# Queueing each operation one step after what it needs, loading tiles' y a slot sooner, and padding pools so that weights lie 64 bytes above

## The chip, the cores and the metric

The kernel runs on one core of a Trainium2 chip. The metric is the time of one execution on the device, in microseconds (us). The engines are named as the profile names them: PE is TensorE's matmul, PEld its weight load, DVE is VectorE, ACT is ScalarE, POOL is GpSimd, SP is SyncE, which here only issues DMAs.

## The reference, cut to what matters

Three blocks follow each other on an input of 4 x 3072 x 256 floats: a Fourier filter along the sequence, a channel mix with a token shift, and a gated layer of width 2048.

```python
X = np.fft.rfft(x, axis=1); Xr, Xi = X.real, X.imag
Yr = Xr @ w_r - Xi @ w_i + b_r
Yi = Xr @ w_i + Xi @ w_r + b_i
Yr = np.sign(Yr) * np.maximum(np.abs(Yr) - 0.01, 0.0)     # and Yi the same
y = np.fft.irfft(Yr + 1j * Yi, n=3072, axis=1)

prev = y moved one token down
xk = mu_k * y + (1 - mu_k) * prev;  xr = mu_r * y + (1 - mu_r) * prev
k = np.maximum(xk @ w_k, 0.0)
z = (1 / (1 + np.exp(-(xr @ w_r)))) * (k * k @ w_v)

h = z.reshape(12288, 256) @ w_in
out = (h * np.clip(h + 3, 0, 6) / 6) @ w_out
```

## The kernel before

**Products.** Every fp32 operand is split into a high part `h` (ACT copies it to the rounded type fp32r) and a low part `l` (DVE subtracts `h`); `three` then issues three matmuls for each product. A matmul has a stationary operand (the "weights" of the PE, 128 columns, loaded by a LDWEIGHTS ahead of it) and a moving one of 192, 256 or 512 columns. Either can be a tensor of weights of the model or data.

**Order.** All engines' queues are written out by hand: each engine executes its instructions in the order in which the program text issues them, and waits in that order. The Fourier filter is a stream of steps (generators that yield): `s1` and `mid` (which for each of 12 column groups j runs `s2`, `mix` and `ia`, through DRAM in between) and `ib`. After a first stretch with the stream alone, the channel mix runs beside it: per tile of 512 tokens one unit `u_r` and four `u_k`, each `u_k` followed two units later by its `u_v`; between units `feed` takes one step of the stream, and `ahead` prepares the next tile: it issues `load_y` (DMA of the tile's y), and takes steps of `prep` (ACT scales the shifted tokens into `xf`, DVE adds the others, ACT and DVE split it into `kh`, `kl`). A tile has ten slots. When the stream is empty the channel mix runs alone, and `decoder` steps decode the last block's weights: weights arrive as 64 bit floats and are turned into fp32 by DVE (L196, L200 to L204) and ACT (L197, L198), then split. L196 makes what L197 reads, and both are issued in the same step.

**Soft threshold.** `mix` ends with three DVE instructions on 128x512: add the bias (L361), `min(y + 0.01, 0)` (L362), `max(y - 0.01, that)` (L363); `split_y` and `ia` follow one step of j later.

**Last block.** The first tile (i = 0) runs in units `u_i` (12 matmuls of 512 columns, a gate on ACT and DVE, a split) and, three units later, `u_o` (24 matmuls of 256 columns). Beside them, from j = 3 on, `sums` and `split_s` prepare sums of weights (tile `sw`) and of data (tiles `th`, `tl`). The other 23 tiles run in 184 units `u_s` of 45 matmuls of 256 columns: 21 of a seven-product scheme into `rq` and `cc`, with `sw` or `wi` stationary, in four pieces with the 24 matmuls of an earlier unit's `u_o` between them. Into `oacc` the data `gh`, `gl` are stationary and the weights `wo` move.

**Where tiles lie.** Pools are laid out tile after tile, at 32 byte steps: `cst`, `kb`, `kw` (later `sp`) from the left, `fp` (later `w2`) up to the right end. Almost all tiles are multiples of 256 bytes long per partition, so a tile's offset modulo 256 is its pool's. In the program of the kernel before it is 32 for all of `kb`, `kw` and `sp`, 224 for all of `fp` and `w2`, 128 for `f1` and `fi`. The offset of the stationary operand less that of the moving one, modulo 256, is then 64 for `oacc` (`gh` 32, `wo` 224), 192 for products with `wi` stationary, and 0 for those with `sw`, for `mix`, `s2` and `ia`, and for the products `pr`, `pk` and `acc` of the channel mix.

Of the kernel before, what the change touches and what calls it, by code (L numbers as in the profile page):

```python
# [9 lines left out]
F32 = mybir.dt.float32  # L10
# [93 lines left out]
def fourier_mix_ffn_kernel(  # L104
# [36 lines left out]

    def ptile(name):
        return ps.tile([128, 1024], F32, tag="h", name=name)
# [15 lines left out]
    class Weights:  # L159
# [24 lines left out]
        def decode(self, staged, k, q, c, m):  # L184
# [3 lines left out]
            if self.wide:  # L188
# [7 lines left out]
                ts(au, high, 20, 0x7FF, op0=ALU.logical_shift_right, op1=ALU.bitwise_and)  # L196
                nc.scalar.activation(f, ai, AF.Relu, bias=top[:, 0], scale=-1.0)  # L197
# [5 lines left out]
                yield  # L203
# [6 lines left out]
            split(f, hi, lo)  # L210

    def decoder(jobs, stage):

        running = []
        for n in range(2 * len(jobs) + 4):
# [7 lines left out]

    def stage1():
        w = kb.tile([128, 1024], U32, tag="gh", bufs=3, name="stw")
        return w, kb.tile([128, 2, TOK], F32, tag="gl", bufs=3, name="stt")

    with tc.manual_schedule(engines=order):
        ff = ctx.enter_context(ExitStack())
        fp = ff.enter_context(tc.tile_pool(name="fp", bufs=1, side="right"))  # L230

        f1 = cst.tile([N1, 2, N1], F32R, name="f1")
        fi = cst.tile([N1, 2, N1], F32R, name="fi")
# [3 lines left out]
        half = cst.tile([128, 1], F32, name="half")  # L237
        top = cst.tile([128, 2, 1], F32, name="top")
        bias = fp.tile([128, 3, D], F32, name="bias")
# [9 lines left out]

        def load_chunks(upto):  # L250
            while head["load"] < min(len(chunks), upto) and chunks[head["load"]][1] in ready:
                n = head["load"]
                src, _, p = chunks[n]
                a = fp.tile([128, 2, D], F32, tag="a", bufs=5, name="a")
# [48 lines left out]
        def load_t(b, j):  # L303
# [3 lines left out]
            if b < B:  # L307
                t = fp.tile([128, 2, 640], F32R, tag="t", bufs=3, name="tt")
# [4 lines left out]
        def mid(b):  # L313
# [31 lines left out]
            def mix(j):  # L345
                xh, xl = xx.pop(j)
                p = ptile("mix")
                for g in range(2):
# [6 lines left out]
                    three(p[:, 256 * g : 256 * g + 256], pairs)  # L355
                y = fp.tile([128, 512], F32, tag="y", bufs=2, name="yf")
# [23 lines left out]

            for j in range(NP + 1):
                if j < NP:
                    s2(j)
# [5 lines left out]
                if j:  # L389
                    mix(j - 1)  # L390
                    fetch()
                    yield
                if 2 <= j < NP:
                    ia(j - 2)

# [72 lines left out]
        nc.vector.memset(half, 0.5)  # L468
        nc.vector.memset(top[:, 0], 1170.0)
        nc.vector.memset(top[:, 1], 254 * 2.0**23)  # L470

        def vectors():
# [7 lines left out]
            nc.vector.tensor_scalar(omu, mus, -1.0, 1.0, op0=ALU.mult, op1=ALU.add)  # L480

# [10 lines left out]
        def prep(i):  # L492
# [9 lines left out]
            for w in (1, 0):  # L502
# [14 lines left out]
                nc.scalar.activation(h, xf, AF.Copy)  # L517
                nc.vector.tensor_sub(l, xf, h.bitcast(F32))  # L518
# [74 lines left out]
        def u_i(i, j):  # L593
# [13 lines left out]
            split(g, h, l)  # L607
# [74 lines left out]
        def u_s(sp, pz, i, j, other, before, aside):  # L682
# [13 lines left out]
            cut = [len(other) * n // 3 for n in range(4)]  # L696
# [132 lines left out]
        for _ in range(3):  # L829
            next(preps)  # L830
            next(preps)
            next(fs)
# [20 lines left out]
        done2 = 0  # L853

# [7 lines left out]
        def ahead(i, slot):  # L862

            nonlocal preps
# [121 lines left out]
```

## Time and profile before

| | us |
|---|---|
| median of 3 runs | 2080.52 |
| lowest, highest | 2079.47, 2082.42 |
| the profiled execution | 2082.47 |
| its span, first to last instruction | 2080.7 |

The span is 1.8 us less than the profiled execution's own time, and that execution took 2.0 us more than the median. Times in the rows are counted from the span's start. Three stretches follow each other: the Fourier stream alone to about 170 us, stream and channel mix to about 780 us, the channel mix alone to about 1055 us, then the last block.

### The profile page before, as it was taken

How to read it: one execution, taken by the hardware profiler on the slowest of the kernel's cores; microseconds unless marked ns; L12 is line 12 of the kernel's file. 1: busy time of each engine (PE TensorE's matmuls, PEld its weight loads, DVE VectorE, ACT ScalarE, POOL GpSimd, SP SyncE). 2: the span in 40 equal slices, each digit the busy share in tenths (PEclk: the TensorE clock that was granted, in tenths of full speed). 3: DMA queues.
4: the chain of work that ended last, by engine and by line, in shares of the span. 5: the costliest groups of instructions: out<-in, count | busy, mean ns of one | idle time of the engine just before them, and what ended most of it. 6: DMA issues, size and time to landing. Idle time of an engine off the chain costs nothing.

```text
span 2080.7 us, 33798 instructions
## 1 busy us (share of the span) xinstructions
PE 1992.8 (96%) x13928; PEld 1844.5 (89%) x13928; DVE 1549.8 (74%) x1975; ACT 1323.2 (64%) x1917; POOL 35.0 (2%) x63
## 2 busy tenths in 40 slices
PE   6878999999999999889998999999999999999998
PEld 4867998898789888667787999999999999999998
DVE  3868667777677686767777777877787778777875
ACT  5556447555754565555646777777777777667775
POOL 0000000000000000000000000000000000000000
PEclk7978999999999999999999999999999999999999
DMA  9765447543653352122100001100110011001100
GB/s 265 240 205 165 123 114 228 163 142 115 216 170 111 95 179 65 63 75 77 51 31 24 29 23 29 32 21 23 30 32 21 22 31 32 21 22 31 32 11 21
DMA packets 106988, 175.85 MB, mean 85 GB/s; under 512 B 12945, under 2 KB 63314, under 8 KB 106834
## 3 DMA queue, kind: packets, MB, share of 16 engines
q1 hardware_dynamic: 96034, 141.76, 22.1%
q0 software_dynamic: 10480, 31.67, 5.7%
q8 instruction: 109, 1.79, 0.4%
q14 instruction: 45, 0.37, 0.1%
q10 hardware_dynamic: 320, 0.26, 0.0%
HBM read 110.35 MB, written 63.31 MB: 83 GB/s over the span
## 4 chain that ended last, share of the span: by engine, by line
PE 76%; DVE 14%; ACT 6%; issue 2%; DMA 2%; SPq 0%; ACTq 0%; DVEq 0%
PE oacc L776 24%; PE rq L776 15%; PE acc L156 8%; PE pk L156 7%; PE cc L776 6%; PE mix L156 5%; PE s L156 4%; DVE g L552 2%; DVE gl L553 2%; PE pr L156 2%; DVE xf L511 1%; PE ia L156 1%; DVE kl L518 1%; PE ib L421 1%; PE ib L420 1%
## 5 line engine op out<-in xcount | busy, mean ns | idle before, releaser
L776 PE MATMUL oacc<-wo_hi,gl 128*128 128x256 f32 x1536 | 426.7, 278 | 0.6 <-DVE gl L750 0.6
L776 PE MATMUL oacc<-wo_hi,gh 128*128 128x256 f32 x1536 | 427.1, 278 | 0.0
L776 PE MATMUL oacc<-wo_lo,gh 128*128 128x256 f32 x1536 | 425.4, 277 | 0.0
L776 PEld LDWEIGHTS oacc<-wo_hi,gl 128*128 128x128 f32 x1536 | 288.7, 188 | 1.0 <-DVE gl L750 0.8
L776 PEld LDWEIGHTS oacc<-wo_hi,gh 128*128 128x128 f32 x1536 | 288.5, 188 | 0.2
L776 PEld LDWEIGHTS oacc<-wo_lo,gh 128*128 128x128 f32 x1536 | 288.7, 188 | 0.0
L732 DVE TENSOR_TENSOR c<-rq,s 128x512 f32<-128x512 f32 x184 | 127.3, 692 | 184.2 <-ACT s L728 184.2
L745 DVE SCALAR_TENSOR_TENSOR g<-g,c 128x1024 f32<-128x1024 f32 x184 | 225.5, 1226 | 27.1 <-ACT g L744 17.4
L749 ACT ACTIVATE gh<-g 128x1024 fp32r<-128x1024 f32 x184 | 195.2, 1061 | 55.8 <-DVE g L745 55.8
L750 DVE TENSOR_TENSOR gl<-g,gh 128x1024 fp32r<-128x1024 f32 x184 | 223.7, 1216 | 1.2 <-ACT gh L749 1.2
L776 PE MATMUL rq<-th,sw 128*128 128x256 f32 x1104 | 217.4, 277 | 7.3 <-DVE g L606 7.3
L744 ACT ACTIVATE g<-c,half 128x1024 f32<-128x1024 f32 x184 | 211.5, 1150 | 4.1 <-DVE c L733 1.4
L712 ACT ACTIVATE s<-rq 128x512 f32<-128x512 f32 x184 | 109.9, 598 | 112.0 <-PE rq L776 111.5
L776 PEld LDWEIGHTS rq<-th,sw 128*128 128x128 f32 x1104 | 166.4, 188 | 7.5 <-DVE g L606 7.5
L156 PE MATMUL acc<-gl,wv_hi 128*128 128x512 f32 x384 | 153.8, 400 | 13.3 <-DVE gl L553 13.3
L547 ACT ACTIVATE g<-pk 128x1024 f32<-128x1024 f32 x96 | 97.6, 1016 | 106.5 <-PE pk L156 106.4
L156 PE MATMUL pk<-kh,wk_hi 128*128 128x512 f32 x384 | 152.8, 398 | 9.3 <-ACT kh L517 5.2
L776 PE MATMUL rq<-tl,sw 128*128 128x256 f32 x552 | 153.9, 279 | 2.8 <-DVE tl L679 2.8
L148 DVE TENSOR_TENSOR al<-a,ah 96x512 fp32r<-96x512 f32 (+1 forms) x176 | 114.9, 684 | 55.2 <-ACT ah L147 55.2
L156 PE MATMUL acc<-gh,wv_hi 128*128 128x512 f32 x384 | 153.2, 399 | 1.6 <-ACT gh L551 1.5
L156 PE MATMUL acc<-gh,wv_lo 128*128 128x512 f32 x384 | 152.2, 396 | 0.0
L156 PE MATMUL pk<-kl,wk_hi 128*128 128x512 f32 x384 | 151.9, 396 | 0.0
(150 smaller groups left out, 4953.0 us busy)
## 6 DMA issues: line engine op xcount, KB each, us to landing
tt<-in_tab_dram POOLq DMA_DIRECT2D x40, 640.0 KB, 4.9
yt<-sc_y SPq DMA_DIRECT2D x23, 608.0 KB, 3.9
a<-in_x_dram SPq DMA_DIRECT2D x64, 192.0 KB, 3.5
sc_a<-s1sb SPq DMA_DIRECT2D x32, 384.0 KB, 3.9
a<-sc_a SPq DMA_DIRECT2D x48, 256.0 KB, 3.2
sc_b<-iasb SPq DMA_DIRECT2D x48, 256.0 KB, 4.8
a<-sc_b SPq DMA_DIRECT2D x64, 192.0 KB, 3.1
sc_y<-ysb SPq DMA_DIRECT2D x32, 384.0 KB, 2.9
```

The lines of the kernel that those rows point to most:

```text
L148: nc.vector.tensor_sub(l, src, h.bitcast(F32))
L156: nc.tensor.matmul(o, a, c, start=first and i == 0, stop=last and i == n - 1, **kw)
L547: nc.scalar.activation(g, p, AF.Relu)
L552: nc.vector.tensor_mul(g, g, g)
L553: nc.vector.tensor_sub(l, g, h.bitcast(F32))
L712: nc.scalar.activation(s[:, 1:3].rearrange("p a n -> p (a n)"), rq, AF.Copy)
L732: nc.vector.tensor_add(c[:, 1::2], two(rq), s[:, 0:2])
L744: nc.scalar.activation(g, c, AF.Relu, bias=half, scale=1.0 / 6.0)
L745: nc.vector.scalar_tensor_tensor(g, g, 1.0, c, op0=ALU.min, op1=ALU.mult)
L749: lambda: nc.scalar.activation(h, g, AF.Copy),
L750: lambda: nc.vector.tensor_sub(l, g, h.bitcast(F32)),
L776: return lambda: nc.tensor.matmul(o, lhs, rhs, start=start, stop=stop, skip_group_check=True)
```

## The change

1. `decode`: L196 has a step of its own, the two ACT instructions come a step after it, the multiplication L204 moves up to the step of L200 to L202, and the split's ACT and DVE halves come in two steps. A job takes one step more.
2. `mix`: 0.01 is taken off the bias once, at the start; L362 becomes an ACT Relu with a bias tile (`lam2`), issued after `fetch`, and L363 moves to the start of the next j.
3. `prep`: the split's DVE half is a step of its own, so a tile takes 8 steps instead of 6. `load_y` is issued in slot 9 of the tile before where its y is written already, and the 8 steps then begin in slot 0 (to slot 7); otherwise as before.
4. First tile of the last block: the new sums of data come first, some DVE work (`between`) is put between the ACT and DVE halves of `u_i`'s split, part of the sums moves behind j = 7, and the last decode steps and `sp` stand ahead of `u_i` at j = 3. In the first `u_s`, all 24 matmuls of `u_o` come ahead of the 21.
5. `pad`: unused tiles of 32 to 192 bytes in the pools. Added up, they put `kb`'s `gh`, `gl` at 32, its other tiles (`xf` to `yt`) at 160, `wr`, `wk` and `sw` at 224, `wv` at 96, `th`, `tl` at 160, `f1` at 160, `fi` at 32, `a`, `ah`, `al`, `ev` at 96, `tt`, `Xh`, `Xl` at 32; `wi`, `wo`, `aw`, `yh`, `yl` stay at 224. For every product of high parts the stationary operand then lies 64 above the moving one, modulo 256.

```diff
 class Weights.decode
                 ts(au, high, 20, 0x7FF, op0=ALU.logical_shift_right, op1=ALU.bitwise_and)
+                yield
                 nc.scalar.activation(f, ai, AF.Relu, bias=top[:, 0], scale=-1.0)
                 nc.scalar.activation(ai, f, AF.Relu, bias=top[:, 1], scale=-(2.0**23))
                 yield
                 stt(au, high, 0x80000000, au, op0=ALU.bitwise_and, op1=ALU.bitwise_or)
                 ts(high, high, 0xFFFFF, 0x100000, op0=ALU.bitwise_and, op1=ALU.bitwise_or)
                 stt(f, low, 2.0**-32, high, op0=ALU.mult, op1=ALU.add)
-                yield
                 nc.vector.tensor_mul(f, f, a)
...
             yield
-            split(f, hi, lo)
+            nc.scalar.activation(hi, f, AF.Copy)
+            yield
+            nc.vector.tensor_sub(lo, f, hi.bitcast(F32))
 mid
                 nc.vector.tensor_add(y, p[:, 0:512], bs.rearrange("p g d -> p (g d)"))
-                nc.vector.tensor_scalar(m, y, LAM, 0.0, op0=ALU.add, op1=ALU.min)
-                nc.vector.scalar_tensor_tensor(y, y, LAM, m, op0=ALU.subtract, op1=ALU.max)
                 yy[j] = (y, yh, yl)
+                yield
+                nc.scalar.activation(m, y, AF.Relu, bias=lam2, scale=-1.0)
+                yield
+                nc.vector.scalar_tensor_tensor(y, m, -1.0, y, op0=ALU.mult, op1=ALU.max)
...
+            rest = iter(())
             for j in range(NP + 1):
+                next(rest, None)
                 if j < NP:
                     s2(j)
...
                 if j:
-                    mix(j - 1)
+                    rest = mix(j - 1)
+                    next(rest)
                     fetch()
+                    next(rest)
                     yield
 prep
                 nc.scalar.activation(h, xf, AF.Copy)
+                yield
                 nc.vector.tensor_sub(l, xf, h.bitcast(F32))
 ahead
-            if slot == late and i + 1 < len(seq):
-                b, t = seq[i + 1]
-                drain(b, (TOK * t + TOK - 1) // N1 // 4 if t else 0)
-                load_y(i + 1)
-                preps = prep(i + 1)
-            elif slot >= late + 2:
-                next(preps, None)
+            if i + 1 < len(seq) and i not in begins and (i + 1 in yt or slot == late):
+                begins[i] = (0, 8) if i + 1 in yt else (late + 2, 10)
+                if i + 1 not in yt:
+                    drain(*chunk(i + 1))
+                    load_y(i + 1)
+                preps, left = prep(i + 1), 8
+            if left and slot >= begins[i][0]:
+                for _ in range(-(-left // (begins[i][1] - slot))):
+                    next(preps, None)
+                    left -= 1
+            if slot == 9 and i + 2 < len(seq) and ("y", *chunk(i + 2)) in ready:
+                load_y(i + 2)
 u_i
-            split(g, h, l)
+            nc.scalar.activation(h, g, AF.Copy)
+            for f in between:
+                f()
+            nc.vector.tensor_sub(l, g, h.bitcast(F32))
 u_s
-            cut = [len(other) * n // 3 for n in range(4)]
+            cut = [len(other) * n // 3 for n in range(4)] if (i, j) > (1, 0) else [0, 0, 0, 0]
+            if (i, j) == (1, 0):
+                for f in other:
+                    f()
 the first tile of the last block
+                    x1 = split_s(sp, 1)
+                    beside = {
+                        3: ([x1[0][0]], [x1[0][1]]),
+                        4: ([x1[1][0]], [x1[1][1], c0[0][0]]),
+                        5: ([x1[2][0]], [c0[1][0]]),
+                        6: ([c1[0][0]], [c0[1][1], c0[2][0]]),
+                        7: ([c1[1][0]], [c1[1][1]]),
+                    }
-                    beside = {3: c0[:2], 4: c0[2:] + c1[:1], 5: c1[1:], 6: x1[:2], 7: x1[2:] + c2[:1]}
 start
+            nc.vector.tensor_scalar(bias, bias, LAM, None, op0=ALU.subtract)
 pads
+    def pad(pool, n):
+        pads.append(n)
+        pool.tile([128, n // 4], F32, name=f"pad{len(pads)}")
...
+        pad(cst, 32)
+        pad(cst, 128)
+        pad(cst, 64)
+            padded.append(pad(kb, 128))
+        pad_a, pad_t, pad_y = [128], [192], [192]
+        pad(kw_p, 64)
+        pad(kw_p, 128)
+                    pad(sp, 64)
+                    pad(sp, 192)
```

## Rows read from the trace of the kernel before

**Rows 1.** The page: busy time of each engine, share of the span, instructions.
```profile
PE 1992.8 (96%) x13928; PEld 1844.5 (89%) x13928; DVE 1549.8 (74%) x1975; ACT 1323.2 (64%) x1917; POOL 35.0 (2%) x63
```
**Rows 2.** Stretches: length, busy PE, PEld, DVE, ACT, POOL, then clock, DMA.
```profile
52.00:123.00 71.00, 62.43 (x484) 58.43 (x482) 64.02 (x105) 36.94 (x61) 7.74 (x13) 0.99 0.73 223
123.00:208.00 85.00, 67.90 (x324) 57.61 (x324) 60.97 (x96) 58.00 (x94) 1.61 (x3) 0.74 0.61 187
208.00:780.00 572.00, 567.47 (x3370) 500.15 (x3370) 413.06 (x542) 332.40 (x476) 21.39 (x37) 0.99 0.50 151
780.00:1092.00 312.00, 290.60 (x1289) 235.33 (x1287) 229.68 (x283) 175.60 (x208) 0.00 (x0) 0.98 0.19 60
1092.00:1107.00 15.00, 4.91 (x29) 4.41 (x28) 11.34 (x18) 6.32 (x8) 0.00 (x0) 0.69 0.13 35
1107.00:2071.00 964.00, 964.00 (x8311) 964.00 (x8309) 751.26 (x902) 685.17 (x1033) 0.00 (x0) 1.00 0.09 25
```
**Rows 3.** Waits, 780 to 1092 us: who for whom, us, times, longest.
```profile
ACT stt L197 <- DVE stt L196: 67.3, 16, 6.2
...
PE acc L156 <- DVE gl L553: 13.3, 14, 2.0
...
PE pk L156 <- ACT kh L517: 5.2, 1, 5.2
```
**Rows 4.** Timeline, 838 to 847 us: start, length, what, idle before and releaser.
```profile
838.88 0.72 ACT L197 ACTIVATE stt<-stt,top 128x512 f32<-128x512 int32 x1 [4.64 <-DVE stt L196]
...
843.48 1.23 DVE L552 TENSOR_TENSOR g<-g 128x1024 f32<-128x1024 f32 x1 [3.43 <-ACT gh L551]
...
846.02 0.50 PE L156 MATMUL acc<-gl,wv_hi 128*128 128x512 f32 x1 [1.79 <-DVE gl L553]
```
**Rows 5.** Timeline of ACT, 118 to 142 us.
```profile
123.53 0.72 ACT L197 ACTIVATE stt<-stt,top 128x512 f32<-128x512 int32 x1 [3.49 <-DVE stt L196]
```
**Rows 6.** Groups of instructions, 52 to 123 us: busy, mean ns, idle before.
```profile
L362 DVE TENSOR_SCALAR ym<-yf 128x512 f32<-128x512 f32 x12 | 5.2, 430 | 0.4
L197 ACT ACTIVATE stt<-stt,top 128x512 f32<-128x512 int32 x6 | 4.3, 724 | 15.5 <-DVE stt L196 15.5
```
**Rows 7.** The chain that ended last, 20 to 60 us.
```profile
42.69 0.09 DVE omu L480
```
**Rows 8.** DMA issues: form, count, KB, us to landing.
```profile
yt<-sc_y SPq DMA_DIRECT2D x23, 608.0 KB, 3.9
```
**Rows 9.** Waits of PE, 1092 to 1107 us.
```profile
PE rq L776 <- DVE g L606: 7.3, 1, 7.3
PE rq L776 <- DVE tl L679: 2.8, 1, 2.8
```
**Rows 10.** The chain that ended last, its longest pieces.
```profile
201.57 2.87 PE mix L156 x24
...
768.11 2.79 PE acc L156 x12
```
**Rows 11.** Timeline of PE, 1200 to 1206 us: one unit, and the next one's start.
```profile
1200.06 0.39 PE L776 MATMUL rq<-th,sw 128*128 128x256 f32 x2
...
1200.41 0.28 PE L776 MATMUL rq<-xh,wi_hi 128*128 128x256 f32 x1
...
1201.35 0.28 PE L776 MATMUL cc<-tl,wi_hi 128*128 128x256 f32 x1
...
1205.28 0.39 PE L776 MATMUL rq<-th,sw 128*128 128x256 f32 x2
```
**Rows 12.** Timeline of PE, 2066 to 2071.9 us: first and last of 17 matmuls.
```profile
2069.98 0.28 PE L776 MATMUL oacc<-wo_hi,gh 128*128 128x256 f32 x1
...
2071.79 0.28 PE L776 MATMUL oacc<-wo_hi,gl 128*128 128x256 f32 x1
```
**Rows 13.** Timeline of PE, 1068 to 1072 us: first and last of 24 matmuls.
```profile
1068.68 0.28 PE L776 MATMUL oacc<-wo_hi,gh 128*128 128x256 f32 x1
...
1071.39 0.28 PE L776 MATMUL oacc<-wo_lo,gh 128*128 128x256 f32 x1
```

More of the change, by code (lines that the diff above doesn't have):

```diff
@@ L222, in decoder @@
             yield
+    padded = []
     def stage1():
         w = kb.tile([128, 1024], U32, tag="gh", bufs=3, name="stw")
-        return w, kb.tile([128, 2, TOK], F32, tag="gl", bufs=3, name="stt")
+        t = kb.tile([128, 2, TOK], F32, tag="gl", bufs=3, name="stt")
+        if not padded:
+            padded.append(pad(kb, 128))
+        return w, t
     with tc.manual_schedule(engines=order):
@@ L394, in mid @@
                     ia(j - 2)
+            next(rest, None)
             def end(j):
@@ L591, in split_2, with u_i @@
             xt[i] = (h, l)
-        def u_i(i, j):
+        def u_i(i, j, between=()):
             xh, xl = xt[i]
@@ L828, in fourier_mix_ffn_kernel @@
         preps = prep(0)
-        for _ in range(3):
+        for n in range(4):
             next(preps)
             next(preps)
-            next(fs)
+            if n < 3:
+                next(fs)
         units = []
@@ L853, in fourier_mix_ffn_kernel @@
         done2 = 0
+        left = 0
         def decode_to(n):
@@ L862, in ahead @@
         def ahead(i, slot):
-            nonlocal preps
+            nonlocal preps, left
             if i + 1 == len(seq):
@@ L923, in fourier_mix_ffn_kernel @@
             if i == 0:
-                decode_to(max(done2 + 2, 2 * (j // 2 * 2 + 1) + 6, 2 * (8 + j) + 6))
-                u_i(i, j)
+                decode_to(max(done2 + 2, 2 * (j // 2 * 2 + 1) + 7, 2 * (8 + j) + 7))
+                if j == 3:
+                    decode_to(len(wi.jobs + wo.jobs) * 2 + 5)
+                    stage.close()
+                    sp = ctx.enter_context(tc.tile_pool(name="sp", bufs=1))
+                    pad(sp, 64)
+                    sw = [sp.tile([128, 4, 8, 128], F32R, name=f"sw{c}") for c in range(2)]
+                    pad(sp, 192)
+                    c0, c1, c2, c3 = (sums(sp, c) for c in range(4))
+                    x1 = split_s(sp, 1)
[6 more added lines that the diff above has]
+                    }
+                    both = lambda f, g: lambda: (f(), g())
+                    aside = [(both(c1[2][0], c2[0][0]), None), c2[1], (both(c2[2][0], c3[0][0]), None)] + c3[1:]
+                u_i(i, j, beside[j][0] if j >= 3 else ())
                 if lag:
@@ L932, in fourier_mix_ffn_kernel @@
                         f()
-                if j == 3:
-                    decode_to(len(wi.jobs + wo.jobs) * 2 + 4)
-                    stage.close()
-                    sp = ctx.enter_context(tc.tile_pool(name="sp", bufs=1))
-                    sw = [sp.tile([128, 4, 8, 128], F32R, name=f"sw{c}") for c in range(2)]
-                    c0, c1, c2, c3 = (sums(sp, c) for c in range(4))
-                    x1 = split_s(sp, 1)
-                    beside = {3: c0[:2], 4: c0[2:] + c1[:1], 5: c1[1:], 6: x1[:2], 7: x1[2:] + c2[:1]}
-                    aside = c2[1:] + c3
                 if j >= 3:
-                    for on_vector, on_scalar in beside[j]:
-                        on_vector()
-                        if on_scalar:
-                            on_scalar()
+                    for f in beside[j][1]:
+                        f()
             else:
```

17 lines of the change are left out of this document (15 added, 2 removed).

## The prediction

> **What bounds the kernel now.** The page's first part comes first: PE is busy for 96% of the span, DVE for 74%, ACT for 64% [rows 1]. That is an average over stages, so the stretches come next [rows 2]. From 1107 to 2071 us PE never pauses: only the pitch of its matmuls counts there. From 208 to 780 us it pauses for 4.5 of 572 us, so again the pitch. From 780 to 1092 us it is idle for 312 - 290.6 = 21.4 us though DVE is busy for 74% and ACT for 56%: nobody is full, so somebody stands in a queue for the wrong thing. From 52 to 123 us PE is idle for 8.6 of 71 us while DVE is busy for 90%. From 1092 to 1107 us PE works 4.9 of 15 us, at a granted clock of 0.69.
>
> The waits say where the 21.4 us come from [rows 3]: PE waits for DVE's `gl` (13.3 us) and once for `kh` (5.2 us), but the longest line is ACT waiting 67.3 us in 16 pieces for L196. The timeline shows that these are one thing [rows 4]. ACT stands 4.64 us at L197 until L196, the last thing in DVE's queue, is done; the Square behind it, which depends on nothing of the decoder, is late; DVE then stands 3.43 us for that Square; PE stands 1.79 us for the `gl` that follows. The two queues block each other in turn.
>
> **The change, part by part.**
>
> *Decode steps.* L196 goes into a step of its own. The instructions are the same; one order changes, 25 times. ACT's wait at L197 should go, and with it what stands behind it. In the stretch from 780 us the gain lies between 0 (the stall moves to another pair) and 21.4 us (all idle time of PE). DVE needs 229.7 us there [rows 2]; if PE's 21.4 us went, it would be 79% busy, so DVE has room. The single 5.2 us also belongs here: ACT's `kh` was queued behind L197. I take 16: some queueing stays at 79%. Between 123 and 208 us the first lines of PE's idle 17.1 us begin the same way: ACT stands 3.49 us at L197 [rows 5], ahead of the `yh` that the last `ia` of the first `mid` needs. I take 4, between 0 and 8; the rest is a DMA round trip through DRAM and a start at half clock. Staging buffers are held one step longer; a step lasts several us here, so the load's own time stays covered.
>
> *Soft threshold.* 48 times a DVE instruction of 0.430 us goes and an ACT instruction comes. Its nearest row is L197, a Relu on 128x512 with a bias tile, 0.724 us [rows 6]: 48 x 0.430 = 20.6 us off DVE, 48 x 0.724 = 34.8 us onto ACT. The Trainium skill speaks against this (ScalarE: Activation LUTs, Rules for kernel authors: relu, max and min belong on VectorE). The trace agrees on the single instruction, 0.724 against 0.430 us; by that rule alone the change would be worth -14 us of engine time. The sum goes by which engine is full: between 52 and 123 us DVE is at 90% and ACT at 52%, so 12 x 0.430 = 5.2 us come off the busiest queue. I take 5, between 0 (the latency from `mix` to `yl` sets the pace) and 8.6 (all idle). After 208 us, ACT gets 35 x 0.724 = 25 us on 332 of 572 us, and PE covers it. The new Relu waits for DVE's add, and behind it in ACT's queue stand `iasb` and the next unit's `g`; both need matmuls that PE does after `mix`, so they lose nothing while ACT keeps up; without that cover each Relu costs its 0.724 us. L363 stands ahead of the next `s2`, still a step before `split_y` needs it. The subtraction from the bias falls on the path: it follows `omu`, which is on the chain that ended last [rows 7], and `split` waits behind it. 768 elements by the row for 512: at most 0.430 x 1.5 = 0.65 us. I take -0.6.
>
> *Loads of y, and `prep`.* 23 DMAs of 3.9 us [rows 8] are issued one slot sooner on SP. No wait of PE is for `yt`; the 5.2 us wait was counted above. I cost it at nothing: `prep` begins a slot later and covers it; uncovered, each load would cost up to 3.9 us. SP may stand one slot longer for the store of the last y chunk, with loads of `a` queued behind it; five buffers of `a` cover that. The split into two steps takes DVE's wait for `kh` away and is in the terms above.
>
> *First tile of the last block.* PE's wait of 7.3 us for DVE's `g` and 2.8 us for `tl` [rows 9], and the slow clock that follows them, are the cost now. The gate itself is one instruction on ACT and one on DVE, each about as long as the 1.23 us of DVE's 128x1024 in [rows 4], and 24 products run beside them; so the 7.3 us are DVE's queue of sums, not the gate. The change takes two of DVE's sums behind j = 7, computes `tl` first, fills DVE's wait for `gh` with sums, and puts 24 matmuls (24 x 0.118 = 2.8 us) in front of what waits. At least these 2.8 us are covered; at most 10.1 us of waits and 4.9 x 0.31 = 1.5 us of slow clock. I take 9, since nothing but the gate should be left in front.
>
> *Pads.* Matmuls of one shape, 256 columns, do not run at one pitch. `mix`, stationary and moving at the same offset modulo 256 (difference 0): 2.87 / 24 = 119.6 ns [rows 10]. Products with `wi` (difference 192): 0.94 us over 8 steps, 117.5 ns [rows 11]. `oacc` (difference 64): 1.81 us over 16 steps, 113.1 ns [rows 12]. So where operands lie seems to matter, and 64 is the best seen. But the evidence is not clean: the same `oacc` products ran at 2.71 / 23 = 117.8 ns behind matmuls of 512 columns [rows 13]. For 512 columns, 2.79 / 12 = 232.5 ns [rows 10], about twice 113.1 and no room to gain: I put 0 there, at most 6 ns each.
>
> A unit `u_s` takes 1205.28 - 1200.06 = 5.22 us [rows 11], 116.0 ns on average over 45. With all at 113.1 it takes 5.09 us: 184 x 0.13 = 24 us gained. With all at 117.8, 5.30 us: 184 x 0.08 = 15 us lost. The pads leave `oacc` at its 64, and the six changes per unit between `oacc` and the scheme keep other differences (128 and 0), so not all 24 come: I take 12. For `mix` between 208 and 780 us (35 x 24 products): 840 x 6.5 ns = 5.5 us at most, with `ia` 1 more; at 117.8 ns, 1.5. I take 4, plus 1 for the waits in that stretch.
>
> What speaks against it: the Trainium skill (TensorE: Matmul & The Clock Gate, Step-by-step) says that PE reads moving and stationary operands through two independent ports, so that loading the next weights takes nothing from the running matmul. By that rule the pads do nothing; rows 10 to 12 disagree with it, rows 13 leave it open. It is the first rival.
>
> **The sum**, against the profiled execution's 2082.5 us: 16 + 4 + 5 - 0.6 + 9 + 12 + 5 = 50.4, so 2032 us. Against the median, 2 us lower, it would be 2030; I stay at 2032.
>
> **The rivals.**
>
> *The pads do nothing.* Pitch then depends on which matmuls come before, as rows 13 allow, and 12 and 4 fall away: 2048 us. For it: 117.8 and 113.1 ns on the same addresses. Against it: `mix` never leaves 119.6 at difference 0, and `oacc` holds 113 through long runs.
>
> *The stalls only move.* ACT still waits, now for L202's step or for the `xf` that DVE adds; of 16 + 4 + 5 only 5 come: 2052 us. For it: DVE also waits for ACT, as in the second line of [rows 4]. Against it: that line is itself an echo of L197, which is the longest wait of the stretch by far.
>
> *Everything comes.* 21.4 + 8 + 8.6 - 0.6 + 11.6 + 24 + 11 (5.5, 1 and the 4.5 of idle PE) = 84: 1998 us. It needs both the differences of 128 and 0 to be harmless and DVE never to be late.
>
> *Slower.* One mechanism, in the last block: the changes between differences 64, 128 and 0 throw PE into the slow pitch at every piece. The other gains are 16 + 4 + 5 - 0.6 + 9 = 33.4 us, and there are 184 x 45 = 8280 products, so it decides from 33.4 / 8280 = 4.0 ns more than 116.0, that is 120.0 ns on average, what `mix` has now. At 121 ns the time is 2082.5 - 33.4 + 41.4 = 2090 us.
>
> **How the numbers follow.** The forecast has 0.42, the pads without effect 0.25 (2048), stalls that move 0.14 (2052), everything 0.13 (1998), slower 0.06 (2090). The predicted time is the forecast's, 2032. The range from 2005 to 2060 holds the forecast with its bounds, both middle rivals and, of "everything", the part above 2005; outside stay some 0.18: most of "everything" and the slower case. A change of 0.2%, 4 us, is about the least that a measurement of this kernel tells from none. All cases but one end below 2076; for mixtures of rivals (pads that cost what half the stalls give) I keep 0.03 within 0.2%. So faster 0.90, same 0.03, slower 0.07.
>
> **What would show it.** Each step has its place: between 780 and 1092 us ACT's line for L196 should be nearly gone and PE's idle time down to about 5 us; between 52 and 123 us the steps of j should come every 5.5 instead of 6 us; the wait for `g` before the first `rq` should be under 2 us; a unit `u_s` should take 5.15 us, `mix` 2.75. If `u_s` still takes 5.22 us the pads failed; if PE's idle time after 780 us is 15 us or more, the order did.

## The result, and the profile after

The changed kernel takes 2059.4 us (median of 4 runs, 2058.5 to 2063.9), the kernel before 2081.4 us (2079.5 to 2082.4) beside it: a ratio of 0.9899, 95% interval 0.9884 to 0.9914. The change gains 22 us; the forecast was 50. The time lies in the range, 0.6 us from its upper end.

The page's first part of the changed kernel, PE's line, answers to [rows 1]:

```profile
PE 2000.5 (97%) x13928; PEld 1848.1 (90%) x13928; DVE 1529.6 (74%) x1929; ACT 1353.3 (66%) x1965; POOL 34.6 (2%) x63
```

PE has the same 13928 matmuls, a span 22 us shorter, and is busy for 7.7 us more. The stretches of the changed kernel, with the columns of [rows 2]:

```profile
52.00:123.00 71.00, 60.67 (x471) 58.76 (x470) 55.52 (x88) 43.03 (x72) 7.01 (x12) 0.93 0.67 209
123.00:208.00 85.00, 73.14 (x359) 61.12 (x358) 66.72 (x103) 62.83 (x101) 2.33 (x4) 0.80 0.67 208
208.00:780.00 572.00, 569.27 (x3384) 496.12 (x3383) 396.50 (x507) 357.74 (x511) 21.39 (x37) 1.00 0.49 150
780.00:1092.00 312.00, 306.94 (x1467) 252.20 (x1466) 255.08 (x320) 190.93 (x231) 0.00 (x0) 1.00 0.20 64
1092.00:1107.00 15.00, 14.85 (x127) 14.65 (x125) 13.79 (x19) 11.49 (x19) 0.00 (x0) 1.00 0.01 2
1107.00:2050.00 943.00, 943.00 (x8011) 943.00 (x8010) 722.44 (x861) 659.83 (x995) 0.00 (x0) 1.00 0.09 25
```

From 780 to 1092 us PE's idle time falls from 21.4 to 312 - 306.94 = 5.1 us, and from 1092 to 1107 us from 10.1 to 0.15. From 52 to 123 us it rises, from 8.6 to 10.3, though DVE is busy 8.5 us less. And in the last stretch PE never pauses in either kernel, but does 8011 products in 943 us where it did 8311 in 964: 8.50 in a microsecond, not 8.62.

The stretches are fixed in time, while the work moves through them. Between the same matmuls of both traces (times from the span's start):

| from the start of ... to ... | before, us | after, us | gained | forecast |
|---|---|---|---|---|
| the span, 12th `mix` (end of the first `mid`) | 115.8 | 119.9 | -4.1 | 4.4 |
| 13th `mix` | 85.6 | 78.0 | 7.6 | 4 |
| 48th `mix` (pitch of 208 to 780 us) | 510.5 | 506.7 | 3.7 | 5 |
| first `pi` (decode steps) | 340.4 | 321.8 | 18.6 | 16 |
| first `rq` of the second unit (first tile) | 59.1 | 47.8 | 11.3 | 9 |
| the end (183 units) | 969.3 | 984.4 | -15.0 | 12 |
| sum | 2080.7 | 2058.6 | 22.1 | 50.4 |

Two rows have the wrong sign. The last is one number 183 times. PE's timeline of the changed kernel, one unit and the next one's start, as in [rows 11]:

```profile
1202.16 0.40 PE L824 MATMUL rq<-th,sw 128*128 128x256 f32 x2
...
1203.58 0.28 PE L824 MATMUL oacc<-wo_hi,gh 128*128 128x256 f32 x1
...
1204.40 0.28 PE L824 MATMUL oacc<-wo_hi,gl 128*128 128x256 f32 x1
...
1207.46 0.40 PE L824 MATMUL rq<-th,sw 128*128 128x256 f32 x2
```

The unit takes 5.30 us, where it took 5.22, and `oacc`, whose addresses differ by 64 as before, runs at 0.82 / 7 = 117 ns, the pitch of [rows 13] and not that of [rows 12]. Of the 0.08 us that a unit lost, 0.06 are those of `oacc`: from the 21st unit on its 24 products take 117.5 ns on average where they took 114.9, though the pads left both of its operands where they were, modulo 256.

The first row shows in the waits of 52 to 123 us of the changed kernel:

```profile
ACT ym L391 <- DVE yf L388: 26.3, 8, 4.6
PEld mix L163 <- DVE yf L388: 9.7, 5, 2.1
PE mix L163 <- DVE yf L388: 8.8, 5, 2.0
```

and in one of these five waits, in the timeline from 96 us (DVE's rows from 98 to 102 us, the last product of `ia` among them, then the rows of ACT and PE that wait; the rest left out):

```profile
98.25 0.68 DVE L219 TENSOR_TENSOR wk_lo<-stt,wk_hi 128x512 fp32r<-128x512 f32 x1
98.86 0.68 DVE L208 SCALAR_TENSOR_TENSOR stt<-stw,stt 128x512 uint32<-128x512 uint32 x1
...
99.01 0.28 PE L163 MATMUL ia<-yl,tt 128*128 128x256 f32 x1
...
99.57 0.43 DVE L209 TENSOR_SCALAR stw<-stw 128x512 uint32<-128x512 uint32 x1
100.04 0.69 DVE L210 SCALAR_TENSOR_TENSOR stt<-stw 128x512 f32<-128x512 uint32 x1
100.76 0.69 DVE L211 TENSOR_TENSOR stt<-stt 128x512 f32<-128x512 f32 x1
101.37 0.42 DVE L203 TENSOR_SCALAR stt<-stw 128x512 uint32<-128x512 uint32 x1
101.71 0.68 DVE L388 TENSOR_TENSOR yf<-mix,bias 128x512 f32<-128x512 f32 x1
...
102.43 0.72 ACT L391 ACTIVATE ym<-yf,lam 128x512 f32<-128x512 f32 x1 [4.64 <-DVE yf L388]
102.45 0.39 PE L163 MATMUL mix<-aw_hi,Xh 128*128 128x256 f32 x1 [1.84 <-DVE yf L388]
...
103.06 0.58 ACT L407 ACTIVATE iasb<-ia 128x512 f32<-128x512 f32 x1
```

All six DVE operations of the decode stand in a row for 3.5 us. A new weight enters the decoder every second step, and the order before spread these operations over both of the two; queued one step later, those of a weight (L208 to L211) meet the remainder of the weight ahead (L219) and the first operation of the weight behind (L203), and the next step has none. `mix`'s addition L388 stands behind them, ACT stands 4.64 us at the new Relu L391 with an eviction (L407) behind it, and PE waits 1.84 us. The stall of L197 was taken away and another put in its place, in one stretch.

### The profile page after: what moved, and what is told of

The parts are those of the page before. It is cut to its first block, busy times and chain, and to the rows that moved or that the text cites. A ratio compares the mean times of both kernels' runs of the same rounds, so it can differ in the third digit from the quotient of the medians.

```text
span 2058.6 us, 33814 instructions
## 1 busy us (share of the span) xinstructions
PE 2000.5 (97%) x13928; PEld 1848.1 (90%) x13928; DVE 1529.6 (74%) x1929; ACT 1353.3 (66%) x1965; POOL 34.6 (2%) x63
## 4 chain that ended last, share of the span: by engine, by line
PE 80%; DVE 10%; ACT 5%; DMA 3%; issue 1%; SPq 0%; ACTq 0%; DVEq 0%
PE oacc L824 25%; PE rq L824 15%; PE acc L163 9%; PE pk L163 8%; PE cc L824 6%; PE mix L163 5%; PE s L163 4%; PE pr L163 2%; DVE g L591 2%; DVE gl L592 1%; PE ia L163 1%; PE ib L454 1%; PE pi L163 1%; PE ib L455 1%; DVE xf L549 1%
## 5 line engine op out<-in xcount | busy, mean ns | idle before, releaser
L824 PE MATMUL oacc<-wo_hi,gl 128*128 128x256 f32 x1536 | 431.6, 281 | 0.5 <-DVE gl L798 0.5
L824 PE MATMUL oacc<-wo_lo,gh 128*128 128x256 f32 x1536 | 430.4, 280 | 0.0
L824 PEld LDWEIGHTS oacc<-wo_hi,gh 128*128 128x128 f32 x1536 | 293.1, 191 | 0.2
L824 PE MATMUL rq<-th,sw 128*128 128x256 f32 x1104 | 222.1, 284 | 0.8 <-ACT s L771 0.6
L591 DVE TENSOR_TENSOR g<-g 128x1024 f32<-128x1024 f32 x96 | 117.4, 1222 | 79.8 <-ACT gh L590 79.8
L163 PE MATMUL pk<-kh,wk_lo 128*128 128x512 f32 x384 | 151.6, 395 | 0.0
```

The costliest lines, as they stand in the source:

```text
L163: nc.tensor.matmul(o, a, c, start=first and i == 0, stop=last and i == n - 1, **kw)
L591: nc.vector.tensor_mul(g, g, g)
L824: return lambda: nc.tensor.matmul(o, lhs, rhs, start=start, stop=stop, skip_group_check=True)
```

## Experiments

Each kernel was timed in turn with the kernel before on the same chip (medians 2081.5 to 2082.2 us); ratios are to that kernel.

### Order and pads apart

The new order with every tile at its offset of before: every pad 0 (and one of 224 bytes behind the constants, so that they take what they took).

```diff
-            padded.append(pad(kb, 128))
+            padded.append(pad(kb, 0))
...
-        pad_a, pad_t, pad_y = [128], [192], [192]
+        pad_a, pad_t, pad_y = [0], [0], [0]
...
-                    pad(sp, 64)
+                    pad(sp, 0)
```

> The new order alone, every tile at the offset it had before. Theory 1 (the pads cost): the pads lengthen a unit of the last block from 5.22 to 5.30 us (184 x 0.08 = 15 us) and the 512-column products from some 229 to 234 ns (2592 x 4.6 ns = 12 us), and give 1152 x 5.6 ns = 6 us back in mix; so this takes 2059 - 21 = 2038 us, a unit 5.22 us. Rival (the slow pitch comes from the new order of the first units of the last block, offsets do nothing): 2059 us, a unit 5.30 us.

The old order with the changed kernel's pads:

```diff
+            padded.append(pad(kb, 128))
...
+        pad(cst, 32)
         f1 = cst.tile([N1, 2, N1], F32R, name="f1")
...
+                    pad(sp, 64)
                     sw = [sp.tile([128, 4, 8, 128], F32R, name=f"sw{c}") for c in range(2)]
```

> The kernel before with the pads and nothing else. Theory 1: 2081 + 21 = 2102 us, a unit 5.30 us, mix at about 115 ns. Rival: 2081 us, a unit 5.22 us, mix at 120 ns.

The new order with the pads of the constants and of the first pool (`fp`) alone:

```diff
-            padded.append(pad(kb, 128))
+            padded.append(pad(kb, 0))
...
-        pad(kw_p, 64)
+        pad(kw_p, 0)
...
-                    pad(sp, 64)
+                    pad(sp, 0)
```

> The new order with the pads of cst and fp alone, so that mix, s2, ia and ib keep their difference of 64 and the channel mix and the last block lie as before. Theory 1: 2059 - 15 - 12 = 2032 us, a unit 5.22 us, mix at 115 ns. Rival: 2059 us.

The kernel just above, with the last block's stationary operands all at 32 and its moving operands all at 224 modulo 256 bytes (shown against the changed kernel; the channel mix has difference 0 throughout):

```diff
-            padded.append(pad(kb, 128))
+            padded.append(pad(kb, 192))
...
+                    pad(w2, 192)
                     wo = Weights(w2, w_out, 16, D, "wo")
```

> As the run with the pads of cst and fp alone, but in the last block every stationary operand lies at 32 and every moving one at 224, so the difference is 64 also where PE goes from one kind of product to the other; the channel mix has difference 0 throughout. If what spoils the last block are the differences of 128 and 0 at these changes: a unit of 45 x 113.3 = 5.10 us and 2032 - 22 = 2010 us. If a difference of 64 has two pitches whatever precedes it, and the last block settles in the slow one: a unit of 5.30 us and 2047 us.

The new order alone: 2044.6 us, 0.9817 (0.9799 to 0.9834), a unit at 5.220 us (PE's timeline, the starts of two units):

```profile
1202.47 0.39 PE L825 MATMUL rq<-th,sw 128*128 128x256 f32 x2
...
1207.69 0.39 PE L825 MATMUL rq<-th,sw 128*128 128x256 f32 x2
```

The pads alone: 2097.4 us, 1.0070 (1.0055 to 1.0085), a unit at 5.300. So the order gains 37 us and the pads lose 15 to 16, with either order; theory 1 had the pads at 21. With the pads of the first pool alone: 2041.0 us, 0.9801 (0.9787 to 0.9816): only those pay, by 3.6 us. `mix` has difference 64 in this kernel as in the changed one, and the mean from start to start after 200 us is 117.8 ns here and 114.4 there: one pair of addresses, two pitches, as in [rows 12, 13].

The fourth kernel was expected at 2010 us and took 2055.9, 0.9872 (0.9854 to 0.9890). Its first whole unit took 5.101 us, all products at 113.3 ns. In each of the next three PE waited once, for 0.2 to 0.5 us, and each wait turned the pitch over: 117.7 ns behind the first, 113.3 behind the second, 117.7 behind the third and from there to the end, every unit 5.300 us. Two waits in the opening unit, whose 24 `oacc` come ahead of its other 21 products, had left it at 113.3. PE's timeline, the starts of the first two whole units and then the three waits (the first one without a gap of its own: the second product of that row comes 0.22 us behind the first):

```profile
1070.72 0.39 PE L825 MATMUL rq<-th,sw 128*128 128x256 f32 x2
...
1075.83 0.39 PE L825 MATMUL rq<-th,sw 128*128 128x256 f32 x2
...
1078.17 0.50 PE L825 MATMUL rq<-th,sw 128*128 128x256 f32 x2
...
1085.60 0.51 PE L825 MATMUL rq<-th,sw 128*128 128x256 f32 x2 [0.21 <-ACT s L772]
...
1089.63 0.50 PE L825 MATMUL rq<-th,sw 128*128 128x256 f32 x2 [0.23 <-ACT s L761]
```

Differences of 128 and 0 between the pieces, my suspicion in the forecast, are gone here, and the slow pitch is not.

### What sets the pitch

The body of the kernel was replaced by series of products that nothing waits for:

```diff
+        for d in range(0, 64, 8):     # floats: differences 0, 32, ... 224 bytes
+            series(d, 512, 24, p); series(d, 256, 40, p)
+            for r in range(4):        # a wait for ACT, then
+                series(d, 256, 40 + r, p)
+            series(d, 192, 24, q)
```

> The body of the kernel is replaced by series of products that nothing waits for: stationary and moving operands whose addresses differ by 0, 32, 64, ... 224 bytes modulo 256, and for each difference 24 products of 512 columns, straight behind them 40 of 256, four more series of 40 to 43 of 256 each behind a wait of PE for ACT, and 24 of 192; nothing of the reference is computed. Theory A (the pitch is a matter of the difference and of how a series began): at difference 64 the products of 256 columns take 113.3 ns in some of the series and 117.7 in others, each the same from its beginning to its end, and at difference 0 they take 119 to 120; products of 512 columns take 229 ns at some differences and 234 at 64. Rival B (the two pitches belong to the order of the last block's products, not to the operands): every series of one difference has one pitch, 113 or 118 ns.

PE's timeline of it, a whole series in one row (start, time from the first start to the last end, what, count), first difference 0, then 64:

```profile
29.29 5.60 PE L150 MATMUL five<-mov,wts 128*128 128x512 f32 x24
34.73 4.95 PE L150 MATMUL run<-mov,wts 128*128 128x256 f32 x40
...
104.39 5.79 PE L150 MATMUL five<-mov,wts 128*128 128x512 f32 x24
110.02 4.87 PE L150 MATMUL run<-mov,wts 128*128 128x256 f32 x40
...
115.88 4.76 PE L150 MATMUL rs0x<-mov,wts 128*128 128x256 f32 x40
...
121.63 5.04 PE L150 MATMUL rs1x<-mov,wts 128*128 128x256 f32 x41
...
127.66 5.16 PE L150 MATMUL rs2x<-mov,wts 128*128 128x256 f32 x42
...
133.81 5.10 PE L150 MATMUL rs3x<-mov,wts 128*128 128x256 f32 x43
```

The 42 products of the third series at difference 64 take longer than the 43 of the fourth. Start to start, from the third product on, in ns:

| difference | 0 | 32 | 64 | 96 | 128 | 160 | 192 | 224 |
|---|---|---|---|---|---|---|---|---|
| 256 columns, lowest series | 119.7 | 118.3 | 113.3 | 117.4 | 118.7 | 119.8 | 117.7 | 116.7 |
| 256 columns, highest series | 120.0 | 118.5 | 117.8 | 118.7 | 120.1 | 120.0 | 117.8 | 117.8 |
| 512 columns | 226.7 | 233.4 | 233.4 | 234.3 | 232.4 | 233.8 | 229.5 | 233.5 |

Theory A holds: at 64 a series has 113.3 or 117.8 ns, from its beginning to its end. For 512 columns 64 is no good place: 6.7 ns worse than 0.

Does a product at difference 0 set the good pitch for those behind it, as `sw` seems to before `oacc` in the kernel before? Three kernels: the changed one with the sums back at 0; the best one so far (its decode is told below) with the first products' weights at 64 too; the same with one sum in four at 0.

```diff
-                    pad(sp, 64)
+                    pad(sp, 0)
```

> The changed kernel (2059.4 us) without the two pads of the pool that holds the sums of weights: the 12 products of a unit of the last block that have a sum as stationary operand stand at difference 0 to their moving operand again, the other 33 stay at 64, and nothing else is changed. Theory A: products at difference 0 throw those at 64 that follow into the fast pitch (121.7, 115.8, 114.2, then 113.3 ns, as in the kernel before), so a unit takes 5.18 us (5.16 to 5.20) where it takes 5.30: 2037 us (2033 to 2041). Rival B: the pitch of the others goes by their own operands alone and stays 117.7 ns: a unit takes 5.29 us or more, 2057 us (2054 to 2060).

```diff
+                    pad(w2, 128)
                     wo = Weights(w2, w_out, 16, D, "wo")
```

> As the kernel whose decode is spread further (2026.5 us; a unit of the last block takes 5.220 us with the sums at difference 0, the second products' weights at 64 and the first products' weights at 192), with the first products' weights moved to 64 by one pad of 128 bytes. Theory A: behind the sums they fall into the fast pitch too: a unit takes 5.18 us, 2019 us (2016 to 2023). Rival B: products at 64 that follow other products at 64 stay slow, as in the changed kernel: 5.25 us or more, 2032 us or more.

```diff
-                    sw = [sp.tile([128, 4, 8, 128], F32R, name=f"sw{c}") for c in range(2)]
+                    for c in range(2):
+                        s1 = sp.tile([128, 1, 8, 128], F32R, name=f"sw{c}a")
+                        pad(sp, 64)
+                        sw.append((s1, sp.tile([128, 3, 8, 128], F32R, name=f"sw{c}b")))
```

> As the kernel of theory A just before, and of the four sums only the first stays at difference 0 (three products at the start of a unit), the other three move to 64: 42 of a unit's 45 products are at 64. Theory A: three products at 0 are enough to set the fast pitch once in every unit: 5.12 us (5.11 to 5.15), 2009 us (2005 to 2015). Rival B: three are not enough, or the first wait behind them sets the slow pitch again: 5.25 to 5.30 us, 2032 to 2041 us.

Measured: 2058.5 us, 0.9884 (0.9870 to 0.9899), a unit at 5.280; 2025.2, 0.9724 (0.9708 to 0.9740), at 5.233; 2026.0, 0.9732 (0.9711 to 0.9754), at 5.227. The first came out at its rival's time; the other two lie between theory and rival, their units nearer to the rival's 5.25 us. Products behind a sum at 0 fell to 113.3 ns in some pieces of the unit and stayed at 117.6 in others, always the same pieces. My theory fell; what the pieces differ in is where both operands lie before and behind the step. So the unit's 45 products were run in their order, without waits, for 48 choices of places:

```diff
+        # moving: x at a, wo at 0; stationary: sums at a + ds, wi at a + dw, h at 64
+        for ds, dw in ((0, 192), (0, 64), (64, 64), (64, 192), (192, 64), (128, 64)):
+            for a in range(0, 256, 32):
+                for half in range(2):      # a wait of PE between the halves
+                    for u in range(3):
+                        unit(a, (a + ds) % 256, (a + dw) % 256, rq, cc, o, u == 0, u == 2)
```

> The body of the kernel is replaced by the 45 products of a unit of the last block in their order, for 48 choices of where the operands lie modulo 256 bytes, three units straight on and three more behind a wait of PE; nothing of the reference is computed. Theory C (the step of both operands' places from one product to the next sets the pitch, not the difference alone): the third unit of a choice takes the same time before and behind the wait, the five choices that ran in the kernel come out at 5.22, 5.23, 5.28, 5.30 and 5.10 or 5.30 us as there, and some other choice gives 5.15 us or less. Rival D (other work of the kernel sets the pitch: PSUM, the evictions of ACT, the waits): the five do not come out as in the kernel, and choices of one set of differences agree to 0.02 us.

PE's timeline of it: the starts of the second and third unit at the changed kernel's places (x at 192 above `wo`); then at those of the fourth kernel above (x level with `wo`), ahead of the wait and behind it; then with `wi` at 192 instead:

```profile
741.08 0.87 PE L159 MATMUL rq0a192s0w<-mov,wts 128*128 128x256 f32 x6
...
746.38 0.87 PE L159 MATMUL rq0a192s0w<-mov,wts 128*128 128x256 f32 x6
```
```profile
549.03 0.87 PE L159 MATMUL rq0a0s64w<-mov,wts 128*128 128x256 f32 x6
...
554.33 0.87 PE L159 MATMUL rq0a0s64w<-mov,wts 128*128 128x256 f32 x6
...
565.34 0.84 PE L159 MATMUL rq1a0s64w<-mov,wts 128*128 128x256 f32 x6
...
570.44 0.84 PE L159 MATMUL rq1a0s64w<-mov,wts 128*128 128x256 f32 x6
```
```profile
805.48 0.84 PE L159 MATMUL rq0a0s64w<-mov,wts 128*128 128x256 f32 x6
...
810.58 0.84 PE L159 MATMUL rq0a0s64w<-mov,wts 128*128 128x256 f32 x6
```

That is 5.30, then 5.30 and 5.10, then 5.10 us. The places of the kernel before give 5.220, those of the two kernels above 5.280 and 5.233: each as in its kernel. The places alone, with nothing else of the kernel running, give a unit's time in these four kernels, to 0.01 us. Over the 48 choices it goes from 5.10 to 5.32; choices with the same differences (sums at 64, `wi` at 192) reach from 5.10 to 5.31, so the difference of a product's two operands doesn't decide: what the product before it used counts too. `oacc` shows it best: it lies at the same two places in all 48 choices, and its mean pitch goes from 113.3 to 118.0 ns. One choice, that of the fourth kernel, has two times 0.2 us apart, and a wait chose; theory C, by which both should have been the same, misses there. Two other choices gave 5.10 on both sides of the wait; they ran in the kernel:

```diff
-            padded.append(pad(kb, 0))
+            padded.append(pad(kb, 192))
...
+                    pad(w2, 64)
                     wo = Weights(w2, w_out, 16, D, "wo")
...
-                    pad(sp, 0)
+                    pad(sp, 64)
```

> As the kernel whose decode is spread further (2026.5 us, a unit of the last block 5.220 us), with the places of the last block's operands by the series of units: all moving operands at 224, the stationary ones at 32 (sums, second products) and at 160 (first products' weights). Theory C (places alone): a unit takes 5.100 us as in the series, 2004 us (2000 to 2009). Rival D (the kernel's waits and evictions set the pitch too): the first wait sets the slow pitch and it stays, as with all of them at 32: 5.30 us, 2041 us; in between if only a part of the units keeps it.

```diff
-                    pad(w2, 64)
+                    pad(w2, 192)
...
-                    pad(sp, 64)
+                    pad(sp, 192)
```

> The same with the sums at 160 and the first products' weights at 32. Theory C: 5.100 us a unit, 2004 us (2000 to 2009). Rival D: 5.20 to 5.30 us, 2023 us or more.

2013.3 us, 0.9674 (0.9659 to 0.9689), and 2010.7 us, 0.9662 (0.9649 to 0.9675): near theory C, but both above its range. PE's timeline of the second, two units' starts:

```profile
1205.63 0.39 PE L827 MATMUL rq<-th,sw 128*128 128x256 f32 x2
...
1210.73 0.39 PE L827 MATMUL rq<-th,sw 128*128 128x256 f32 x2
```

5.10 us. 136 of its 183 intervals between units are that; the others, most of them 5.15 to 5.30, make the mean 5.130. So theory C holds for three quarters of the units. In most of the rest, 40 units, the weights of the 21st product load late, the start of the 22nd comes 150 to 228 ns behind it, and up to 16 products after that run at 116 ns or more. The 21st product writes `rq` again, and ACT must have copied it out before. In the timeline of all engines:

```profile
1160.91 0.59 ACT L763 ACTIVATE s<-rq 128x512 f32<-128x512 f32 x1
...
1161.55 0.30 PEld L827 LDWEIGHTS rq<-th,sw 128*128 128x128 f32 x2
1161.59 0.47 PE L827 MATMUL rq<-th,sw 128*128 128x256 f32 x2
```

In these 40 units that copy ends 0.05 to 0.13 us before the 21st product starts, in all the others from the sixth on at least 0.24 us before. They are the sixth and seventh unit of the token tiles (one is an eighth), and ACT's instruction just ahead of the copy is a split of the next tile's data. Moving those splits was not tried. This is the fastest kernel of the study, 49 us below the changed one.

### The parts of the order

On the base of the new order with the first pool's pads (2041.0 us), one part each was undone, and in the last kernel the decode was spread further:

```diff
-                yield
                 nc.scalar.activation(f, ai, AF.Relu, bias=top[:, 0], scale=-1.0)
...
+                yield
                 nc.vector.tensor_mul(f, f, a)
...
-            nc.scalar.activation(hi, f, AF.Copy)
-            yield
-            nc.vector.tensor_sub(lo, f, hi.bitcast(F32))
+            split(f, hi, lo)
```

> As the kernel with the new order and the pads of the constants and of the first pool alone (2041.0 us), but the decode of a weight is spread over the steps as before the change (multiplication and split one step later and together). Theory A, a lump: in the new order all six DVE operations of the decode fall into the same step of two, 3.6 us together, and that is what PE's mix products wait for at 52 to 123 us (8.8 us in five waits); the old spread gives these 8 us back and loses the 13 to 16 us that the new one won at 780 to 1092 us and 4 at 123 to 208 us: 2050 us (2046 to 2055), and the waits of the mix products for the addition of the bias go below 3 us. Rival B, the Relu: what delays the addition is the queue on ACT, not the decode; the waits stay and the time is 2058 us (2055 to 2062).

```diff
-                yield
-                nc.scalar.activation(m, y, AF.Relu, bias=lam2, scale=-1.0)
-                yield
-                nc.vector.scalar_tensor_tensor(y, m, -1.0, y, op0=ALU.mult, op1=ALU.max)
+                nc.vector.tensor_scalar(m, y, LAM, 0.0, op0=ALU.add, op1=ALU.min)
+                nc.vector.scalar_tensor_tensor(y, y, LAM, m, op0=ALU.subtract, op1=ALU.max)
```

> As the kernel with the new order and the pads of the constants and of the first pool alone (2041.0 us), but the soft threshold is made as before the change: three DVE operations in the same step, no Relu on ACT. Theory A, a lump of the decode: DVE is late by the same lump and has 0.43 us more of its own in each step; the waits at 52 to 123 us stay: 2043 us (2040 to 2048). Rival B, the Relu: it stands on ACT 26.2 us in front of the evictions and splits behind it, waiting for DVE; without it 52 to 123 us gets back 8 us: 2033 us (2030 to 2037).

```diff
-            for f in between:
-                f()
...
-                u_i(i, j, beside[j][0] if j >= 3 else ())
+                u_i(i, j)
...
-            cut = [len(other) * n // 3 for n in range(4)] if (i, j) > (1, 0) else [0, 0, 0, 0]
+            cut = [len(other) * n // 3 for n in range(4)]
```

> As the kernel with the new order and the pads of the constants and of the first pool alone (2041.0 us), but the first token tile of the last block and the first unit of its second are queued as before the change (sums beside the splits and the split in one piece, the unit's other products shared out over its three gaps). Theory A: the stalls at the start of the second tile (7.3 and 2.8 us before the change) come back and nothing else: 2051 us (2048 to 2054). Rival B: those stalls had been shortened by the decode that ended sooner, and the order of the first tile gave little: 2043 us (2040 to 2046).

```diff
                 stt(f, low, 2.0**-32, high, op0=ALU.mult, op1=ALU.add)
+                yield
                 nc.vector.tensor_mul(f, f, a)
```

> As the kernel with the new order and the pads of the constants and of the first pool alone (2041.0 us), but the multiplication of the decode goes one step later (and the rounding and the remainder behind it one too): DVE has 2.2 us of decode in one step and 1.4 in the next, where it had 3.6 and nothing. Theory A, a lump: the waits of the mix products for the addition of the bias (8.7 us in five) fall below 3 us, and the time to 2034 us (2031 to 2037). Rival B, the Relu on ACT: the waits stay, 2041 us (2039 to 2044).

The decode undone: 2080.6 us, 0.9995 (0.9986 to 1.0004), outside both theories. The waits from 815 to 1065 us in that kernel begin with

```profile
ACT stt L205 <- DVE stt L204: 75.9, 14, 7.0
DVE g L590 <- ACT gh L589: 52.7, 19, 4.6
```

the pair of [rows 3, 4] again, longer than in the kernel before (61.3 and 26.4 us there). Without the decode's new steps the rest of the order and the first pool's pads gain 1 us together: the parts don't add up, and the decode's steps are what lets the others pay. Why the others make its old wait longer stays open.

The threshold undone: 2037.2 us, 0.9774 (0.9758 to 0.9790). The Relu on ACT costs 3.8 us where I had put a gain of 5. The cost is the first `mid`, 116.2 us to the 12th `mix` where it was 122.3: the five waits of `mix` are gone, though the lump of the decode stands as it did. The stretch to the 13th `mix` got longer instead, 82.3 us for 76.6. The first tile undone: 2052.0 us, 0.9853 (0.9838 to 0.9867): 11 us, as theory A had it. The decode spread further: 2026.5 us, 0.9727 (0.9710 to 0.9745), better than theory A's 2034. Its waits from 52 to 123 us, and a stretch of its decode steps (columns as in [rows 2]):

```profile
ACT ym L394 <- DVE yf L391: 23.2, 12, 3.3
PE mix L164 <- DVE yf L391: 3.3, 5, 0.7
```
```profile
780.00:1050.00 270.00, 270.00 (x1240) 224.46 (x1239) 227.42 (x281) 172.91 (x204) 0.00 (x0) 1.00 0.22 70
```

The longest wait of PE for L391 is 0.7 us where it was 1.9, and from 780 to 1050 us PE no longer pauses at all, where it paused for 7.1 us. The lump was costing in both places. The stall of the first `mid` takes both, the lump and the Relu: with either one taken away most of it ends.

## Why the prediction was wrong

*The step that failed* is the pads' 12 us in the last block; it measured -15.0 (-14.2 between the new order alone and the changed kernel, 970.2 and 984.4 us), and with it 27 of the 28 missing us are told. The forecast read the pitch as a matter of the difference, with 64 the best seen, and took half of the gain that 113.1 ns everywhere would give. The runs showed that 64 has two pitches and that the places of the operands from product to product choose between them. [Rows 12, 13] had shown both, and the text had worked out the other end, "With all at 117.8, 5.30 us", to the digit; it then stood in no case. Two pitches on the same addresses were evidence that the difference doesn't decide, and the term should have had both signs, between -15 and 24. That the pads do nothing, the first rival, is refuted too: they move a unit from 5.10 to 5.32 us. The Trainium skill (TensorE: Matmul & The Clock Gate, Step-by-step) says that loading the next weights takes no read bandwidth from the running matmul. As the prediction read that rule the pads would do nothing, and the series of units has 5.10 and 5.30 us on the same products. Whether it is the loading of weights that the places slow is not shown.

*The 512 columns* were put at 0. At the pads' difference of 64 the mean from start to start after 200 us rises from 229.0 to 233.5 ns, 4.5 ns on 2592 products, 12 us. Less than half of it shows in the time; part is made up by shorter waits of PE for `gl` (6.8 and 4.3 us from 200 to 1020 us). Between the new order alone and the changed kernel, the stretch up to the 48th `mix` has 3.0 us more of these products and 4.3 less of `mix` (2.1 gained in all, 508.8 and 506.7 us), and the next stretch is 2.3 us longer. The term of 5 came out at 3.7, 2.1 by the pads and 1.7 by the order. The 232.5 ns of [rows 10] were one of the chain's longest pieces, not the mean.

*Soft threshold*: 5 forecast, 4 lost by the last experiments. DVE was the busiest queue and did get emptier, 55.5 us for 64.0; but the step was not limited by DVE's load, it was limited by who stands behind whom. The Relu puts a wait for DVE into ACT's queue, and the cover I named (both need matmuls that PE does after `mix`) doesn't cover: in the timeline above, `ia` ends at 99.3 us and `iasb` begins at 103.06, behind the Relu. The Trainium skill's rule that relu belongs on VectorE (ScalarE: Activation LUTs, Rules for kernel authors) agrees with the 3.8 us. The reason that it gives is the time of an element; here the waits behind the Relu come with it.

*Right, or near*: decode steps 16 (18.6 between the same matmuls), the first tile 9 (11.3, and 11 by the experiment), loads of y 0 (no wait of PE names `yt`). The decode's other 4 stand against 7.6, but most of that comes only with the new threshold, as its experiment shows. The bias costs 0.09 us in the chain where 0.6 was allowed. Together the order was forecast at 33.4 us and gave 37, in part by luck: in the new order alone the first `mid` lost 4.0 where 4.4 were forecast as a gain, and the four stretches behind it each gained more than forecast. The rival of stalls that only move was true of the first `mid` alone. The slower rival named the effect, a slow pitch in every unit, but priced it at 121 ns; it is 117.7. Its cause, changes between differences, is not what it takes: the fourth kernel has none and is slow too.

## What to carry to other kernels

When the trace shows two durations for one instruction on the same addresses, history decides: take both as bounds with both signs, and measure the sequence by itself before you move tiles; a series without waits gave the unit of four kernels to 0.01 us. When a dependent step is queued one step later to end a stall, write down what every engine then holds in each step: operations that had been spread can meet. And a busy share says which engine is full, not who stands in whose way.

## What was unexpected of the hardware

- Products of 256 columns that follow without a pause run at 113.3 to 120.1 ns by the places of their operands modulo 256 bytes (varied in steps of 32) and by the product before; at difference 64 both 113.3 and 117.8 ns keep themselves up, the slow one in one kernel for every unit from 1.09 ms to the end.
- Products of 512 columns take 226.7 ns at difference 0, 229.5 at 192 and 232.4 to 234.3 elsewhere; products of 192 columns take 111.5 to 111.8 at every difference.
- A wait of 0.2 us of PE can change the pitch of all that follows, by 4%; other waits of that kernel left it as it was.
